# A recurrence with a dense block behind it: TensorE's order of issue mixes two kinds of products, and weights, checks and one inversion move

## The chip, the cores and the metric

The kernel runs on one core of one Trainium2 chip. The metric is the device time of one execution in microseconds (us). Three executions of the kernel before took 703.22, 706.95 and 708.93 us; the median is 706.95 us.

## The reference

For each of 4 batches and 8 heads a 40 x 40 state is carried over 768 time steps; then every token goes through a normalisation and a two-layer block ("MoE" in the names), with a residual:

```
for t in range(768):                       # state: 4 x 8 x 40 x 40, zero at first
    y[t]  = r[t] @ state
    Sa    = state @ a[t]
    state = state * w[t] - outer(Sa, b[t]) + outer(v[t], k[t])
x   = y, heads side by side                # 4 x 768 tokens of 320
xn  = (x - mean) / sqrt(var + 1e-6) * g_ln
out = x + relu(xn @ w_ch1) @ w_ch2         # 320 -> 1280 -> 320
```

All inputs are float32 and so is the output.

## The kernel before, in words

**Chunks.** The 768 steps are cut into 24 chunks of 32 steps. Inside a chunk the recurrence becomes small matrix products per head, all 32 batch-head pairs at once; from chunk to chunk only the state is carried. A chunk's work on TensorE (PE) is a set of small products, each with 32 to 40 columns and often a quarter of the array: `tri` (L424), `pq` (L408) and `kbt` (L531) prepare it, `prh` (L561), `solve` (L576) and `st` (L604) carry the state on, `ss` (L628) and `ut` (L655) transpose, `z` (L672) and `y` (L695) give the chunk's output. VectorE (DVE) runs two scans of the decays per chunk (`g` L367, `q` L376) and evicts results; GpSimd (POOL) scales keys (`kb` L395) and `aT` (L385). The triangular matrices of a slab of 2 or 4 chunks are inverted by forward substitution, row after row (`invert`, L477 to L487): slabs 0 and 1 in two halves of 16 rows on DVE, slab 2 in full on DVE, slabs 3 to 6 in full on POOL. A slab done by halves costs its chunks two more `solve` products and a DVE addition (L583).

**The block.** Two chunks give 256 tokens, a group; there are 12 groups. `norm` makes a group's normalised tokens, split into a high and a low part (transposes `nt`, L878). `moe` runs 10 first products `l1` (L929; 8 matmuls of 256 columns each) and 20 second products `l2` (L906; 3 matmuls of 320 columns each). Between them ScalarE (ACT) writes the high part of the hidden layer (L934) and DVE the low part (L938).

**Weights.** They arrive as 64-bit floats and are turned to a high and a low 32-bit part: ACT shifts the exponent (L748), DVE puts the bits together (L763, L764, L774), POOL multiplies by the sign (L770) and subtracts (L817), in three buffers inside `yi[1]`, the buffer in which POOL later inverts slabs 3 to 6.

**What sets the order.** Every step is a task with its engines, an estimated duration, what it reads and writes, and a due time worked back from the end. `Plan.run` plays all tasks through once before the kernel is built, engine by engine, and always takes the ready task with the smallest key; the result is a fixed list of instructions for each engine. For PE there are two additions. The planner sums an estimate of columns (`USE`) of the products of the last 2.4 planned us; while the sum is under `NEED` (1500) it takes a ready product with over 900 first, which only `l1` and `l2` have. And between 6 and 70 planned us, where nothing is ready, it issues a filler (`unit`, L1048: a product of 160 columns that nobody reads). All DMAs go through SP's queue.

**A check.** `wild` (L362, DVE) collects for each chunk whether any decay lies outside a range; if so, a slow path at the end would redo everything. It isn't taken here.

Of the kernel before, what the change touches and what calls it, by code (L numbers as in the profile page):

```python
# [33 lines left out]
HALVES = (0, 1)  # L34
BY_POOL = (3, 4, 5, 6)
NBK = 7
# [5 lines left out]
SPAN, NEED = 2.4, 1500  # L42
UNITS = (6.0, 70.0)
BACKLOG = 2.0


class Plan:
# [4 lines left out]
    USE = dict(l1=2048, l2=960, nt=384, tri=320, z=320, st=364, prh=480, solve=160, y=520, kbt=100, pq=340, ss=83, ut=80)  # L52
# [7 lines left out]
    def add(self, where, emit, r=(), w=(), shift=0.0, bank=None, of="", kb=0, land=2.2, sort=None, due=None):  # L60

        t = dict(n=len(self.tasks), where=where, emit=emit, shift=shift, due=due, bank=bank, of=of, kb=kb, land=land,
                 deps=set(), sort=sort)
# [16 lines left out]
    def run(self, n_banks=8, unit=None):  # L80
        T = self.tasks
        n = len(T)
        follow = [[] for _ in T]
        left = [0] * n
        uses = {}
        opens = {k: t for t in T for k in t["bank"]}
        for t in T:
            for k in t["ps"]:
                o = opens[k]
                if o is not t:  # L90
                    o["deps"].update(d for d in t["deps"] if d < o["n"])
        for t in T:
            for d in t["deps"]:
                follow[d].append(t["n"])
            left[t["n"]] = len(t["deps"])
            t["uses"] = set()
        for t in T:
            for k in t["bank"]:
                uses[k] = 0
        for t in T:  # L100
            for k in t["ps"]:
                uses[k] += 1
        free = {e: 0.0 for e in self.ENGINES}
        ready = {e: [] for e in self.ENGINES}
        ends = [None] * n
        avail = [0.0] * n
        done = [False] * n
        banks = list(range(n_banks))
        held = {}
        count = {"moe": 0, "po": 0, "small": 0}  # L110
        cap = {"moe": 2, "po": 2, "small": 6}
        wire = [0.0]
        used = []
        events = []
        order = []
        now = 0.0

        def release(t):
            for e, us in t["where"]:
                heapq.heappush(ready[e], (t["key"], t["n"]))  # L120

        for t in reversed(T):
# [5 lines left out]
            late = t["due"] if t["due"] is not None else min((T[f]["late"] for f in follow[t["n"]]), default=END)  # L128
            t["late"] = late - us
            t["key"] = t["late"] + t["shift"]  # L130
        for t in T:
            if left[t["n"]] == 0:
                release(t)
# [1063 lines left out]
```

## Time and profile before

| | us |
|---|---|
| median of 3 runs | 706.95 |
| the profiled execution | 708.33 |
| its span, first to last instruction | 706.2 |
| PE busy | 630.6 |
| DVE busy | 418.3 |
| ACT busy | 297.8 |
| POOL busy | 264.2 |

The profile lists for each engine the time in which at least one of its instructions ran. A busy PE may still be slow: TensorE's clock is granted at one of two levels, 2.4 GHz (1.00 in the rows) or 1.2 GHz (0.50), and the profile gives the mean granted clock of any stretch. Its mean over this execution was 0.788.

### The profile page before, as it was taken

What the parts mean: (1) busy time and instruction counts of PE and PEld (TensorE: products, weight loads), DVE (VectorE), ACT (ScalarE), POOL (GpSimd) and SP (SyncE); (2) the same over time, 40 slices, a digit from 0 to 9 for tenths busy, and PEclk for the clock granted to TensorE, in tenths of its full rate; (3) what the DMA queues carried; (4) which work ended last, traced back from release to release, by engine and by line L of the source; (5) the groups of instructions that cost most, each with busy time, mean ns of one, the idle gap of its engine ahead of it and who ended that gap; (6) DMA issues with size and microseconds to landing.
All of it is one profiled execution on the core that took longest, in us unless ns stands there. A gap on an engine that the chain in (4) does not pass through costs nothing. (4 is left out here: it accounts for less than half of the span.)

```text
span 706.2 us, 29730 instructions
## 1 busy us (share of the span) xinstructions
PE 630.6 (89%) x13026; PEld 585.0 (83%) x13026; DVE 418.3 (59%) x882; ACT 297.8 (42%) x747; POOL 264.2 (37%) x380
## 2 busy tenths in 40 slices
PE   5987788499789999999999899899998998989876
PEld 5987777388678889889889899798898997979866
DVE  8989967978865645563465574474435444354232
ACT  7542356642332742562361552633534534345121
POOL 7653711642169550228462238661156500000000
PEclk9899975559869759756969769588588795896969
DMA  9989758352582883665164681646433434121000
GB/s 198 247 225 242 203 125 164 83 137 69 129 146 65 193 166 88 167 142 147 44 158 107 157 168 49 144 105 145 124 60 96 90 78 97 49 78 44 20 1 21
DMA packets 126646, 84.22 MB, mean 119 GB/s; under 512 B 94896, under 2 KB 104624, under 8 KB 126512
## 3 DMA queue, kind: packets, MB, share of 16 engines
q1 hardware_dynamic: 126512, 82.28, 49.9%
q8 instruction: 103, 1.69, 1.0%
q14 instruction: 31, 0.25, 0.1%
HBM read 56.14 MB, written 18.24 MB: 105 GB/s over the span
## 5 line engine op out<-in xcount | busy, mean ns | idle before, releaser
L938 DVE SCALAR_TENSOR_TENSOR hl<-ps,hh 128x256 fp32r<-128x256 f32 x120 | 50.5, 423 | 123.3 <-ACT hh L934 122.8
L929 PE MATMUL ps<-xh,w 128*128 128x256 f32 x480 | 120.9, 312 | 0.7 <-ACT xh L882 0.6
L934 ACT ACTIVATE hh<-ps 128x256 fp32r<-128x256 f32 x120 | 46.2, 385 | 162.0 <-PE ps L929 158.9
L906 PE MATMUL ps<-w,hh 128*128 128x320 f32 x480 | 109.7, 315 | 0.0
L929 PEld LDWEIGHTS ps<-xh,w 128*128 128x128 f32 x480 | 93.6, 215 | 4.3 <-issue 1.4
L395 POOL TENSOR_TENSOR bk<-bk,gE 112x1024 f32<-112x1024 f32 x24 | 55.7, 2321 | 83.4 <-DVE gE L367 33.1
L906 PEld LDWEIGHTS ps<-w,hh 128*128 128x128 f32 x480 | 79.0, 190 | 0.7
L906 PE MATMUL ps<-w,hl 128*128 128x320 f32 x240 | 74.6, 311 | 0.0
L929 PE MATMUL ps<-xl,w 128*128 128x256 f32 x240 | 73.5, 306 | 0.0
L1048 PE MATMUL ps<-start,ident 128*128 128x160 f32 x376 | 61.1, 322 | 11.3 <-DVE gk L430 6.1
L487 POOL TENSOR_TENSOR yi<-yi,ytmp 128x30 f32<-128x30 f32 (+14 forms) x120 | 67.0, 558 | 9.4
L872 POOL COPY xn<-xn 128x64 f32<-128x64 f32 x15 | 4.7, 312 | 168.5 <-ACT xn L867 167.6
L1048 PEld LDWEIGHTS ps<-start,ident 128*128 128x128 f32 x376 | 57.0, 206 | 12.5 <-DVE gk L430 6.9
L483 POOL TENSOR_TENSOR ytmp<-yi 128x30 f32<-128x30 f32 (+14 forms) x120 | 63.6, 530 | 8.1
L684 DVE TENSOR_TENSOR x5s<-ps,mask 64x256 f32<-64x256 f32 x96 | 40.5, 422 | 29.9 <-PE ps L672 25.0
L614 DVE TENSOR_TENSOR x<-ps,x2s 40x320 f32<-40x320 f32 x92 | 44.9, 488 | 19.2 <-PE ps L604 13.3
L604 PE MATMUL ps<-x,xk 128*40 128x40 f32 (+1 forms) x1472 | 49.7, 238 | 7.0 <-ACT x L591 4.8
L537 ACT COPY xk<-ps 64x320 f32<-64x320 f32 x96 | 40.4, 420 | 32.1 <-PE ps L531 29.4
L604 PEld LDWEIGHTS ps<-x,xk 128*40 128x40 f32 (+1 forms) x1472 | 43.4, 150 | 12.3 <-ACT x L591 7.3
L662 ACT COPY vu<-ps 40x256 f32<-40x256 f32 x96 | 35.2, 367 | 41.4 <-PE ps L655 18.8
L929 PEld LDWEIGHTS ps<-xl,w 128*128 128x128 f32 x240 | 51.8, 216 | 0.3 <-DVE xl L886 0.3
L376 DVE TENSOR_TENSOR_SCAN qE<-wa,last 112x528 f32<-112x528 f32 x24 | 46.7, 1946 | 2.8 <-ACT qc L402 0.9
(118 smaller groups left out, 1227.5 us busy)
## 6 DMA issues: line engine op xcount, KB each, us to landing
wa<-in_et_dram SPq DMA_DIRECT2D x48, 195.2 KB
bk<-in_et_dram SPq DMA_DIRECT2D x48, 192.0 KB
xk<-xk SPq DMA_DIRECT2D x48, 160.0 KB
d_g<-gk SPq DMA_DIRECT2D x48, 128.0 KB
x<-in_vt_dram SPq DMA_DIRECT2D x48, 128.0 KB
d_a<-aT SPq DMA_DIRECT2D x48, 99.0 KB
x2s<-d_a SPq DMA_DIRECT2D x48, 99.0 KB
vu<-in_vr_dram SPq DMA_DIRECT2D x48, 96.0 KB
```

Source lines behind the costliest of these rows:

```text
L376: nc.vector.tensor_tensor_scan(out=flat(qE[R])[:, ::-1], data0=t[R, n:0:-1], data1=flat(last[R])[:, ::-1], initial=0.0, op0=ALU.mult, op1= ...
L395: (nc.gpsimd if e == "POOL" else nc.vector).tensor_tensor(out=kb, in0=kb, in1=gE[R, :, 0:C].unsqueeze(2).broadcast_to([112, 16, 2, C]), op ...
L483: g.tensor_tensor(out=tv, in0=y[:, j + 1:, j:j + 1].broadcast_to([n, m, j]), in1=y[:, j:j + 1, 0:j].broadcast_to([n, m, j]), op=ALU.mult)
L487: g.tensor_tensor(out=yv, in0=yv, in1=tv, op=ALU.add)
L604: nc.tensor.matmul(o[r0:r0 + D, h], lhsT=xk1[FROW[hf], hf, p], rhs=X2[FROW[hf], hf, p, 0:D], start=True, stop=True)
L614: nc.vector.tensor_tensor(out=x2[n][r0:r0 + D, hf, 8 * pp:8 * pp + 8, 0:D], in0=banks[b[name]][r0:r0 + D, 0:CH].rearrange("p (h e) -> p h ...
L684: nc.vector.tensor_tensor(out=x5s[ro:ro + 64, hf, 8 * pp:8 * pp + 8], in0=pz[64 * pp:64 * pp + 64], in1=mask[64 * pp:64 * pp + 64].unsquee ...
L906: nc.tensor.matmul(banks[b[name]][:, 0:CH], lhsT=l[:, us], rhs=ws[f"w2_{f}"][:, y], start=f == 0 and x == 0, stop=f == 9 and x == 2)
L929: nc.tensor.matmul(ph, lhsT=l, rhs=r, start=x == 0, stop=x == 7)
L934: nc.scalar.activation(out=hhs[n], in_=banks[b[name]][:, 0:256], func=AF.Relu)
L938: nc.vector.scalar_tensor_tensor(out=hls[n], in0=banks[b[name]][:, 0:256], scalar=0.0, in1=hhs[n].bitcast(F32), op0=ALU.max, op1=ALU.subtract)
L1048: nc.tensor.matmul(banks[b][:, 0:160], lhsT=ident, rhs=flat(start0)[:, 0:160], start=True, stop=True)
```

## The change: what it does

- **PE's order.** As before, a sum under 1500 takes `l1`, `l2` first. New: a sum over 2500 (`ENOUGH`) takes a ready small product first. In between the key decides. The products `low` (below) count as wide.
- **VectorE's turns with GpSimd.** The planner treats POOL's instructions and some of DVE's (`SHARED`) as users of one port that takes one at a time, and holds a task back until it is free. All chunks may have `aT` and `kb` on DVE or POOL (before: POOL alone from chunk 4 on). A second pass over the plan is written (`PASSES`), but it is set to one.
- **Weights.** The exponent shift goes to PSUM and the bits are put together there; the low part comes from two accumulating products on PE (the weight through the identity or a diagonal of `g_ln`, minus the high part) and an ACT copy. POOL has no part in it any more.
- **Check.** Two ACT instructions per chunk (`far_`) replace `wild`.
- **Slab 2** is inverted by halves (`HALVES`). Slabs 4 and 6 are inverted in `yi[0]` (`BUF`).
- **Fillers** go on to 165 planned us; some loads and clears have an earliest time (`t0`); masks are made with fewer POOL instructions.

PE, late in the kernel (around the seventh group), before: rows of one kernel's order are line, operation, destination and sources, columns; `x_..` is the chunk's state, `ident` a transpose.

```order
L561 MATMUL ps_68<-x_0_90,x2s_92 32x40 x32
L628 MATMUL ps_67<-ident,x_0_90 104x40 x8
L695 MATMUL ps_66<-xk_1_97,x5s 32x40 x32
L576 MATMUL ps_68<-hv_99,tt_111 32x40 x32
L604 MATMUL ps_66<-x_0_90,xk_95 40x40 x16
L655 MATMUL ps_67<-ident,x_0_90 104x32 x8
L655 MATMUL ps_68<-ident,x_0_90 104x32 x8
L604 MATMUL ps_69<-x_0_90,xk_95 40x40 x16
L531 MATMUL ps_70<-ident,bk_83 128x40 x8
L531 MATMUL ps_67<-ident,bk_83 128x40 x8
L878 MATMUL ps_66<-ident,xn_126 128x128 x3
L628 MATMUL ps_68<-ident,x_1_91 104x40 x8
```

The same place in the change (L964 is `l2`; L469, L689, L716, L665 are `pq`, `ss`, `ut`, `st`):

```order
L689 MATMUL ps_67<-ident,x_1_92 104x40 x8
L964 MATMUL ps_72<-w_1_505,hh_134 128x320 x2
L964 MATMUL ps_72<-w_1_505,hl_137 128x320
L469 MATMUL ps_68<-ident,qc 128x104 x4
L964 MATMUL ps_66<-w_2_658,hh_132 128x320 x2
L964 MATMUL ps_66<-w_2_658,hl_135 128x320
L716 MATMUL ps_69<-ident,x_1_92 104x32 x8
L716 MATMUL ps_70<-ident,x_1_92 104x32 x8
L665 MATMUL ps_67<-x_1_92,xk_96 40x40 x16
L665 MATMUL ps_68<-x_1_92,xk_96 40x40 x16
L964 MATMUL ps_72<-w_2_658,hh_132 128x320 x2
L964 MATMUL ps_72<-w_2_658,hl_135 128x320
```

Before, the small products of two chunks stand in one piece, and a group's `l1` and `l2` in another. In the change one or a few `l1` or `l2` stand after every two to five small products.

DVE, slab 2's inversion, before (L483 and L487 are its multiply and add on full rows, L774 and L362 weights and `wild`):

```order
L483 TENSOR_TENSOR ytmp_109<-yi_107 128x58
L487 TENSOR_TENSOR yi_107<-yi_107,ytmp_109 128x29x2
L774 SCALAR_TENSOR_TENSOR yi_108<-r_0_4_844,yi_108 128x256
L367 SCALAR_TENSOR_TENSOR gE<-wa_81,start_79 112x528
L483 TENSOR_TENSOR ytmp_109<-yi_107 128x84
L487 TENSOR_TENSOR yi_107<-yi_107,ytmp_109 128x28x3
L483 TENSOR_TENSOR ytmp_109<-yi_107 128x108
L487 TENSOR_TENSOR yi_107<-yi_107,ytmp_109 128x27x4
L362 SCALAR_TENSOR_TENSOR wild<-wa_82,wild 112x512
L483 TENSOR_TENSOR ytmp_109<-yi_107 128x130
L487 TENSOR_TENSOR yi_107<-yi_107,ytmp_109 128x26x5
```

And in the change (L538, L548 are the multiply and add on halves, L745 and L996 are `z` and the low part of the hidden layer):

```order
L745 TENSOR_TENSOR x5s<-ps_69,mask 64x256
L996 SCALAR_TENSOR_TENSOR hl_136<-ps_72,hh_133 128x256
L538 TENSOR_TENSOR ytmp_110<-yi_108 128x108
L548 TENSOR_TENSOR yi_108<-yi_108,ytmp_110 128x2x9x6
L745 TENSOR_TENSOR x5s<-ps_70,mask 64x256
L538 TENSOR_TENSOR ytmp_110<-yi_108 128x112
L548 TENSOR_TENSOR yi_108<-yi_108,ytmp_110 128x2x8x7
L996 SCALAR_TENSOR_TENSOR hl_137<-ps_68,hh_134 128x256
```

Slab 2 now takes 14 pairs of instructions and not 30, `wild` is gone from between them, and the block's own evictions already run there.

The diff, cut to its core:

```
-HALVES = (0, 1)
+HALVES = (0, 1, 2)
+BUF = (0, 0, 0, 1, 0, 1, 0)
...
-SPAN, NEED = 2.4, 1500
-UNITS = (6.0, 70.0)
+SPAN, NEED, ENOUGH = 2.4, 1500, 2500
+UNITS = (6.0, 165.0)
+SLACK = 0.1
+PASSES, MARGIN = 1, 4.0
...
+    SHARED = ("g", "q", "aT", "kb", "inv", "rs")
...
-                        dry = sum(u for _, u in used) < NEED
-                        for k, i in sorted(q) if dry else ():
+                        use = sum(u for _, u in used)
+                        wide = True if use < NEED else False if use > ENOUGH else None
+                        for k, i in sorted(q) if wide is not None else ():
                             t = T[i]
-                            if not done[i] and avail[i] <= now + 1e-9 and self.USE[t["of"]] > 900:
...
+                            if not done[i] and avail[i] <= now + 1e-9 and (self.USE[t["of"]] > 900) == wide:
+                                if full(t):
                                     continue
                                 got = t
                                 break
...
+                        if port[0] > now + SLACK and (e == "POOL" or e == "DVE" and t["of"] in self.SHARED):
+                            put.append((k, i))
+                            heapq.heappush(events, port[0] - SLACK)
+                            continue
...
+                    if e == "POOL" or e == "DVE" and t["of"] in self.SHARED:
+                        us += max(0.0, port[0] - now)
+                        port[0] = now + us
...
-        def wild_(e, b):
-            (nc.gpsimd if e == "POOL" else nc.vector).scalar_tensor_tensor(
-                out=wild[R], in0=t[R, 0:n].bitcast(U32).rearrange("p (h t) -> p h t", t=33)[:, :, 1:33],
-                scalar=0x3f000000, in1=wild[R], op0=ALU.bitwise_xor, op1=ALU.bitwise_or)
+        def far_(e, b):
+            v = qc[R].rearrange("p (h t) -> p h t", t=C)
+            nc.scalar.activation(
+                out=v, in_=t[R, 0:n].rearrange("p (h t) -> p h t", t=33)[:, :, 1:33], func=AF.Abs, bias=lim[R, 0:1])
+            nc.scalar.activation(
+                out=qc[R], in_=qc[R], func=AF.Relu, bias=lim[R, 1:2], accum_out=far[R, c:c + 1])
...
-        both = [("DVE", 0.72), ("POOL", 1.45)] if c < 4 else [("POOL", 1.45)]
+        both = [("DVE", 0.72), ("POOL", 1.45)]
...
-        u = int(by_pool)
-        yt, tmp = yi[u], ytmp[u]
+        u = BUF[si]
+        yt, tmp = yi[u], ytmp[int(by_pool)]
...
+            def up(e, b):
+                nc.scalar.activation(
+                    out=banks[b[name]][:, 0:n], in_=words(i)[1].bitcast(F32), func=AF.Abs, scale=2.0 ** -111)
+            task("ACT", up, 0.45, r=[("raw", i)], bank=name, of="w")
...
+            def low(e, b):
+                o = banks[b[f"wl{i}"]][:, 0:n]
+                nc.tensor.matmul(o, lhsT=ident if wt else dgs[k], rhs=wf, start=True, stop=False)
+                nc.tensor.matmul(o, lhsT=minus, rhs=ws[tag][:, 0], start=False, stop=True)
+            task("PE", low, 0.8, r=[km, "ident", "gt", "minus", ("wh", tag), ("yi", 1)], bank=f"wl{i}", of="low")
 
             def lo(e, b):
-                t = ws[tag]
-                nc.gpsimd.tensor_tensor(out=t[:, 1], in0=wf, in1=t[:, 0].bitcast(F32), op=ALU.subtract)
-            task("POOL", lo, 0.85, r=[km, ("yi", 1)], w=[("w", tag)], of="w")
+                nc.scalar.copy(out=ws[tag][:, 1], in_=banks[b[f"wl{i}"]][:, 0:n])
+            task("ACT", lo, 0.42, r=[("wh", tag)], ps=[f"wl{i}"], w=[("w", tag)], of="w")
...
```

## Rows read from the trace of the kernel before

**Rows 1.** The page: span, and busy time, share, instructions of three engines.

```profile
span 706.2 us, 29730 instructions
...
PE 630.6 (89%) x13026; PEld 585.0 (83%) x13026; DVE 418.3 (59%) x882; ACT 297.8 (42%) x747; POOL 264.2 (37%) x380
```

**Rows 2.** Three stages: stretch, length, busy us per engine, granted clock, DMA.

```profile
0.00:96.28 96.28, 79.67 (x1336) 75.40 (x1336) 88.10 (x151) 45.51 (x98) 52.87 (x64) 0.96 0.85 214
96.28:161.13 64.85, 49.79 (x1341) 44.19 (x1334) 49.67 (x104) 36.52 (x96) 24.43 (x24) 0.53 0.56 124
161.13:706.20 545.07, 501.10 (x10367) 465.43 (x10366) 280.56 (x629) 215.75 (x554) 186.91 (x292) 0.79 0.44 102
```

**Rows 3.** Same columns: stretches at the low clock after 161 us, eleven in all.

```profile
188.44:205.50 17.06, 10.70 (x171) 9.14 (x172) 12.57 (x41) 6.21 (x15) 5.32 (x14) 0.50 0.85 140
...
290.84:331.80 40.96, 39.30 (x896) 36.14 (x895) 21.24 (x46) 17.91 (x47) 17.99 (x30) 0.50 0.67 154
...
669.72:683.37 13.65, 7.49 (x89) 6.23 (x90) 5.31 (x17) 3.30 (x8) 0.24 (x1) 0.50 0.00 1
sum 228.69, PE 208.64 PEld 186.78 DVE 120.03 ACT 109.37 POOL 70.56; mean PE 18.97 PEld 16.98 DVE 10.91 ACT 9.94 POOL 6.41
```

**Rows 4.** Same columns: stretches at the full clock after 161 us, twelve in all.

```profile
161.13:188.44 27.31, 24.80 (x591) 23.02 (x590) 23.96 (x48) 9.55 (x26) 8.32 (x5) 1.00 0.43 106
...
sum 314.03, PE 292.47 PEld 278.65 DVE 160.53 ACT 106.38 POOL 116.35; mean PE 24.37 PEld 23.22 DVE 13.38 ACT 8.87 POOL 9.70
```

**Rows 5.** PE's timeline: start, duration, instruction; two products, each at both clocks.

```profile
146.30 0.41 PE L929 MATMUL ps<-xh,w1x 128*128 128x256 f32 x1
146.51 0.41 PE L929 MATMUL ps<-xl,w1x 128*128 128x256 f32 x1
...
530.47 0.28 PE L929 MATMUL ps<-xh,w1x 128*128 128x256 f32 x1
530.59 0.28 PE L929 MATMUL ps<-xl,w1x 128*128 128x256 f32 x1
...
539.73 0.80 PE L695 MATMUL ps<-xk,x5s 128*32 128x40 f32 x64
...
555.91 1.29 PE L695 MATMUL ps<-xk,x5s 128*32 128x40 f32 x64
```

**Rows 6.** Fillers alone (L1048): stretch, length, PE busy, PEld busy, clock, DMA.

```profile
78.00:84.00 6.00, 1.71 (x11) 1.23 (x10) 1.00 0.85 281
84.00:96.30 12.30, 5.05 (x32) 4.32 (x32) 1.00 0.45 117
```

**Rows 7.** First products alone (L929), then second products alone (L906), same columns.

```profile
174.80:178.20 3.40, 0.87 (x8) 0.85 (x7) 1.00 0.48 141
...
174.80:178.20 3.40, 1.15 (x6) 0.88 (x6) 1.00 0.48 141
```

**Rows 8.** Groups by line: busy us, mean ns of one, idle before, releasers.

```profile
L362 DVE SCALAR_TENSOR_TENSOR wild<-wa,wild 112x512 uint32<-112x512 uint32 x24 | 19.8, 826 | 0.3 <-DMA wa<-in_et_dram 0.3
...
L483 DVE TENSOR_TENSOR ytmp<-yi 128x30 f32<-128x30 f32 (+14 forms) x30 | 15.4, 515 | 0.2
...
L487 DVE TENSOR_TENSOR yi<-yi,ytmp 64x28 f32<-64x28 f32 (+21 forms) x58 | 21.0, 363 | 2.0
...
L477 DVE TENSOR_TENSOR ytmp<-yi 64x28 f32<-64x28 f32 (+6 forms) x28 | 8.1, 291 | 0.8
...
L402 ACT COPY qc<-qE 104x512 f32<-104x512 f32 x19 | 11.7, 618 | 30.1 <-PE ps L408 15.7 <-DVE qE L376 14.3
```

**Rows 9.** Slab 2's multiplies on DVE: count, ns min/median/max, first and last start.

```profile
L483 DVE TENSOR_TENSOR ytmp<-yi x30: 191/348/1969, 124.1 to 196.7; 128x30 f32<-128x30 f32 x2, 128x58 f32<-128x58 f32 x2, 128x84 f32<-128x84 f32 x2, 128x108 f32<-128x108 f32 x2
```

More of the change, by code (lines that the diff above doesn't have):

```diff
@@ L78, in add, with run @@
         return t["n"]
-    def run(self, n_banks=8, unit=None):
+    def run(self, unit=None):
         T = self.tasks
[L82 to L85, printed above, removed]
         opens = {k: t for t in T for k in t["bank"]}
@@ L91, in run @@
                     o["deps"].update(d for d in t["deps"] if d < o["n"])
+        self.follow = [[] for _ in T]
         for t in T:
             for d in t["deps"]:
[L94 to L120, printed above, removed]
+                self.follow[d].append(t["n"])
         for t in reversed(T):
@@ L127, in run @@
                 us = us * STRETCH + 0.3
-            late = t["due"] if t["due"] is not None else min((T[f]["late"] for f in follow[t["n"]]), default=END)
+            late = t["due"] if t["due"] is not None else min((T[f]["late"] for f in self.follow[t["n"]]), default=END)
             t["late"] = late - us
             t["key"] = t["late"] + t["shift"]
+        best = soon = None
+        self.ends = []
+        for _ in range(PASSES):
+            order, soon = self.lay(soon, unit)
+            end = max(t["end"] for t in T)
+            self.ends.append(round(end, 1))
+            if best is None or end < best[0]:
+                best = end, order, [(t["on"], t["at"], t["end"]) for t in T]
@@ L396, in kb_ @@
                 out=kb, in0=kb, in1=gE[R, :, 0:C].unsqueeze(2).broadcast_to([112, 16, 2, C]), op=ALU.mult)
[L397 to L399 removed]
+        task([("DVE", 1.25), ("POOL", 2.35)], kb_, r=["g"], w=kbk, of="kb")
+        task("ACT", far_, 1.25, r=kw + ["lim"], w=["qc", ("far", c)], of="far")
         def qc_(e, b):
@@ L800, in lo @@
-                def lo(e, b):
-                    for hf, rs in enumerate(rows):
-                        x = w1x[0][:, 640 * hf + CH * i:640 * hf + CH * i + CH]
-                        nc.gpsimd.tensor_tensor(
-                            out=x[64:128], in0=wf[rs], in1=x[rs].bitcast(F32), op=ALU.subtract)
-                task("POOL", lo, 1.7, r=[km, ("yi", 1)], w=[("w", "x", i)], of="w")
+                            nc.scalar.copy(out=x(hf)[rs], in_=x(hf)[0:64])
+                task("ACT", hi, 1.3, r=[km, "gt", ("yi", 1)], w=([("raw", 0), ("raw", 1)] if i == 0 else [])
+                     + [("wh", "x", i)], of="w")
@@ L818, in third @@
-            task("POOL", lo, 0.85, r=[km, ("yi", 1)], w=[("w", tag)], of="w")
-        for i in range(2):
-            first(i)
-            second(i)
-        for i in range(2):
-            third(i)
+                if wt:
+                    nc.scalar.copy(out=t[:, 0], in_=wf)
+                else:
+                    nc.scalar.mul(out=t[:, 0], in_=wf, mul=gt[:, k:k + 1])
+            task("ACT", hi, 0.42, r=[km, "gt", ("yi", 1)], w=[("raw", i), ("wh", tag)], of="w")
+            def low(e, b):
+                o = banks[b[f"wl{i}"]][:, 0:n]
+                nc.tensor.matmul(o, lhsT=ident if wt else dgs[k], rhs=wf, start=True, stop=False)
+                nc.tensor.matmul(o, lhsT=minus, rhs=ws[tag][:, 0], start=False, stop=True)
@@ L827, in weights @@
-            third(i)
+            for _ in one(i):
+                pass
     def norm(g):
```

249 lines of the change are left out of this document (148 added, 101 removed).

## The prediction

> **What bounds the kernel now.** I read the page first [rows 1]: PE is busy in 630.6 of 706.2 us, no other engine in more than 418.3. So PE sets the end, and the question is how fast it runs while it is busy. The busy time of three stages answers that [rows 2]. Up to 96 us DVE is the full engine (88.1 of 96.3 us) and PE runs fillers. From 96 to 161 us the clock is at 0.53 and no engine is full: the first chunks pass through PE, DVE and ACT in turn, while DVE (49.7 of 64.9 us) also inverts slab 2. From 161 us to the end PE is busy in 501 of 545 us, at a mean clock of 0.79. This third stage is the kernel.
>
> The same view, cut where the clock changes, splits it into eleven stretches at 0.50 with 228.7 us, in which PE is busy for 208.6 [rows 3], and twelve at 1.00 with 314.0 us, 292.5 busy [rows 4]. (The few microseconds left are the tail.) The long low stretch from 290.8 to 331.8 us has PE busy in 39.3 of 41.0 us: it isn't idleness that makes it low. What runs in such stretches is the piece of small products of two chunks; the clock comes back with the group's first products. PE's timeline prices the level [rows 5]: the 64 records of one `y` take 1.29 us at 0.50 and 0.80 at 1.00, a ratio of 0.62; the first products start 0.21 us apart at 0.50 and 0.12 at 1.00, a ratio of 0.57.
>
> Where wide and small products alternate, the clock held. From 161.1 to 188.4 us it is full throughout [rows 4]; in one piece of that, 174.8 to 178.2 us, first products take 0.87 and second ones 1.15 of 3.4 us, the rest is small ones [rows 7]. Before 96 us the fillers do the same service: between 78.0 and 84.0 us they fill only 1.7 of 6.0 us, between 84.0 and 96.3 us 5.05 of 12.3, and the clock is 1.00 in both [rows 6]. At 96.3 us they end, and it falls.
>
> **The change part by part.** All sums are against the profiled span of 706.2 us; that execution took 708.3, so 2.1 us lie around the span, and its time is 1.4 us above the median.
>
> *PE's order.* If no low stretch remained after 161 us, the 208.6 busy us in them would shrink by 0.38 of themselves (`y`'s ratio): 79 us, the upper bound. The lower one is no gain from the clock at all, and less than that is a rival below. In the change's order wide products stand after every two to five small ones, but thinner than in the alternating stretch of the trace, where they take 2.0 of 3.4 us: in the rows shown, two small products and one `l2`, and there are places with none for seven or eight small products. I take it that the clock falls in some of them and needs a denser piece to come back, and that a third of the low time stays (about 75 us). Gain: two thirds of 79, **53 us**.
>
> *PE's idle time after 161 us.* It is 20.1 us in the low stretches and 21.5 in the full ones [rows 3, 4]. Of the first, 6.4 us lie in 188.4 to 205.5 and 6.2 in 669.7 to 683.4. The first piece ends when slab 2 comes late: its last multiply starts at 196.7 us [rows 9]. The second is the wait for the last group's normalisation with nothing else left. In the new order nearly two groups of `l1` and `l2` are still to do when the last `y` is issued, and slab 2 is done early, so both have other work over them. I take half of the whole, **21 us**; bounds 0 and 40.
>
> *Slab 2, the check, POOL's weights.* Slab 2 now costs 30 multiplies of 515 ns and 30 adds of about 363 ns on DVE [rows 8], 26 us; by halves it is 14 pairs of about 291 ns each, 8 us. `wild` was 24 times 826 ns, 19.8 us. POOL's weight instructions go, and with them DVE's long cases: a multiply of slab 2 has a median of 348 and a maximum of 1969 ns [rows 9]. After 161 us DVE has room and this is worth nothing by itself. From 96 to 161 us it counts: DVE's busy time is 49.7 of 64.9 us there, and PE's 49.8 busy us at 0.53 would be some 31 under the full clock that the longer fillers bring. The chains from PE to ACT to DVE and back remain. The bounds are 0 and 15 us (64.9 less DVE's 49.7); I take **10**.
>
> *What is added.* Two more `solve` products for each of slab 2's four chunks: 8 at about 0.80 us (they have `y`'s 64 records and 40 columns), **6 us** on a full PE; their copies and additions are covered by `l1` and `l2`. The 24 pairs of `low` replace fillers before 160 us; they cost 0, and if that cover were gone some 13 us, by the filler's 32 records in 5.05 us [rows 6], about 0.16 us each, two records a product of 160 columns, and pairs of 256 to 320 columns. ACT takes 24 times two passes, nearest the copy L402 of 0.62 us [rows 8], 30 us, and some 24 evictions of 0.4 us, 10 us; with 298 us busy now it would be near 340 of some 640 us, so it isn't the bound. Its extra before 130 us can delay the first normalisation; that is inside the 0 to 15. Changing more often between wide and small products costs at most a tenth of a microsecond each time; some fifty more changes, **5 us**. Longer fillers run only where no task was ready in the plan; one that runs late delays a real product by 0.3 us at most each, which I count with those 5.
>
> Sum: 706.2 - 53 - 21 - 10 + 6 + 5 = 633 us of span, and **635 us** with the 2 around it.
>
> **The rivals.**
> *The mix is too thin (the other side).* Then the clock falls between the groups' dense pieces and, what is worse, `l1` and `l2`, which run almost wholly at 1.00 now, are drawn into the low time. The work after 161 us is 292.5 + 0.62 x 208.6 = 422 us at the full clock. With a share f of the busy time low, each us of it doing about 0.57 to 0.62 of the work, it takes 422 / (1 - 0.41 f). With 21 us idle, 11 added and 151 before it, the old 706 is reached at 422 / (1 - 0.41 f) = 523, f = 0.47; the kernel before has 0.42. At f = 0.6 the stage takes 560 and the whole **745 us**. For it: no stretch of the trace has so thin a mix of these very products for long. Against it: the fillers between 78 and 96 us, thinner still in part [rows 6]. Chance 0.12.
> *The chain of chunks becomes the limit.* Each `l1` put between two links of the recurrence delays that link, and PE's list is fixed: where a link is late in fact, everything behind it waits. Then the idle 42 us stay and more of the low time with them, half of it: 706.2 - 40 - 5 + 11 + 2, **674 us**. For it: the plan knows durations only as estimates. Against it: wide work is left until the end, so the chain has slack. Chance 0.13.
> *The clock doesn't follow the order.* If it only followed idleness, the mix would bring none of the 53 us, and the idle time, slab 2 and the additions alone would give 706.2 - 21 - 10 + 11 + 2, **688 us**. The row from 290.8 to 331.8 us, low with 96% busy, speaks against it [rows 3]. Chance 0.05.
> The Trainium skill has that rule: "TensorE: Matmul & The Clock Gate", section "Why this matters for your kernels", says that a drop in throughput is avoided by leaving no idle gaps between bursts of matmuls. By that rule the sum would be the 688 us; the trace doesn't agree, since PE was 96% busy at 0.50, and the measurement decides.
>
> **How the numbers follow.** The forecast, 635 us, is one in which a part of the low time stays; it has a chance of 0.68, and with its bounds it goes from 595 (all 79 us gained, most idle time gone) to 668. Chain 0.13, clock 0.05, too thin 0.12, and 0.02 for nothing moving at all. The range goes from 595 to 695: it takes in the chain and the clock, and leaves out the thin mix, nothing moving, and some 0.05 below 595. About 1% is what a measurement of this kernel can tell from no change. Faster by over 1% (under 700 us): 0.68 + 0.13 + 0.05, 0.86. Slower by over 1%: most of the thin case, 0.11. Within 1%: 0.03.
>
> **What the profile after would show.** The clock after the first `l1` should be full in most stretches, with under 100 us low in all; each group's `l1` and `l2` should be spread over the time of two chunks; `y` should mostly take 0.80 us. PE's idle time after the first `l1` should be near 20 us and not behind slab 2. DVE's busy sum should fall by some 35 us, POOL's too, and ACT's should rise by 30 to 40. The first `l1`, now running at 146 us [rows 5], should come at about 135. The prediction is wrong if the low time is still over 150 us; if PE waits for ACT or DVE within the chain by more than 40 us; or if the first `l1` comes later than 150 us.

## The result, and the profile after

The change makes the kernel faster: four executions took 649.23, 650.84, 658.39 and 659.49 us (median 654.62), beside 702.95 to 708.93 us (median 705.09, four executions) for the kernel before. The ratio is 0.925, 95% interval 0.915 to 0.936. The forecast was 635 us in a range of 595 to 695. Executions of one kernel differ here by 1 to 4% along with the granted clock; the ratios leave the disturbed ones out, so they need not be those of the medians.

The profiled execution took 650.84 us, with a span of 649.1. Of its page, the span, the busy times, the clock in 40 slices and the queue that brings instructions (packets, MB, share):

```profile
span 649.1 us, 30979 instructions
...
PE 591.5 (91%) x13640; PEld 540.3 (83%) x13640; DVE 374.4 (58%) x851; ACT 333.7 (51%) x847; POOL 211.2 (33%) x317
...
PEclk9899898988899887898779999979999998899999
...
q8 instruction: 108, 1.77, 1.2%
```

PE does more instructions (13640 for 13026) in less busy time (591.5 for 630.6 us [rows 1]), and the clock digits stand at 7 to 9 throughout. DVE lost 44 us and POOL 53; ACT gained 36.

The same three stages as [rows 2], same columns (stretch, length, busy per engine, clock, DMA share, GB/s):

```profile
0.00:96.28 96.28, 86.16 (x1217) 77.14 (x1217) 70.55 (x144) 61.94 (x150) 38.31 (x39) 0.95 0.84 214
96.28:161.13 64.85, 57.28 (x1739) 49.76 (x1738) 44.03 (x110) 34.08 (x89) 9.27 (x7) 0.91 0.65 136
161.13:649.10 487.97, 448.05 (x10690) 413.42 (x10689) 259.83 (x598) 237.72 (x609) 163.65 (x271) 0.93 0.52 113
```

The third stage is 57.1 us shorter than the 545.07 of before. In the second the clock is at 0.91 for 0.53 and DVE has 5.6 us less to do. Whether the program is further on by its end, the first `l1` tells. Before, it started at 144.9 us in the trace (the rows at 146 us in the prediction are later records of it; a record is one instruction in the trace); now it starts at 146.5, as PE's first instructions of that line show (count, ns min/median/max, first and last start):

```profile
L987 PE MATMUL ps<-xh,w x2: 415/498/582, 146.5 to 147.1; 128*128 128x256 f32 x2
```

The low stretches after 161 us (as [rows 3]; nine and the tail) and the full ones (as [rows 4]; nine):

```profile
161.00:166.01 5.01, 5.01 (x47) 4.27 (x48) 2.50 (x9) 2.17 (x6) 0.00 (x0) 0.50 0.24 52
...
302.54:316.20 13.66, 11.05 (x204) 9.83 (x192) 5.51 (x11) 6.06 (x15) 11.94 (x22) 0.50 0.72 160
...
sum 64.81, PE 57.23 PEld 51.72 DVE 25.74 ACT 23.66 POOL 21.74; mean PE 5.72 PEld 5.17 DVE 2.57 ACT 2.37 POOL 2.17
```

```profile
428.84:541.48 112.64, 107.21 (x2754) 98.93 (x2753) 64.02 (x155) 63.30 (x162) 43.61 (x81) 1.00 0.59 126
...
sum 423.24, PE 390.95 PEld 361.83 DVE 234.09 ACT 214.19 POOL 141.91; mean PE 43.44 PEld 40.20 DVE 26.01 ACT 23.80 POOL 15.77
```

Busy time at the low clock fell from 208.64 to 57.23 us. At the prediction's 0.38 that is 57.5 us, and the span fell by 57.1. PE's idle time is 423.24 - 390.95 = 32.3 us in the full stretches and 5.8 in the low ones (64.81 - 57.23, less the 1.76 of the tail): 38.1 in all, where [rows 3, 4] have 41.6. So the idle time hardly moved. What ends it did. PE's largest waits after (line, what ended the wait, us in all, times, longest):

```profile
PE ps L637 <- issue: 19.0, 11, 2.6
PE ps L756 <- issue: 5.9, 6, 1.7
PE ps L987 <- issue: 3.6, 3, 1.7
PE ps L485 <- issue: 3.5, 2, 3.1
PE ps L469 <- ACT qc L463: 3.3, 2, 2.6
```

"issue" means that the profile shows nothing that PE waited for. Before, the first of these lines was half as large (L576 is the same product, `solve`):

```profile
PE ps L576 <- issue: 9.6, 8, 2.3
```

Summed over all of PE's gaps of more than 0.25 us in the trace, those without a releaser, called standstills below, rose from 20.9 us (17 gaps) to 35.6 (25), and all others fell from 45.3 us (33 gaps) to 14.1 (10). After 161.13 us alone, standstills rose from 16.6 to 27.3 us and the others fell from 18.8 to 4.8. The timeline shows what a standstill looks like (start, duration, instruction, count, idle before):

```profile
301.61 0.39 PE L987 MATMUL ps<-xh,w1x 128*128 128x256 f32 x1 [1.55 <-issue]
301.83 0.28 PE L987 MATMUL ps<-xl,w1x 128*128 128x256 f32 x1
302.04 0.94 PE L756 MATMUL ps<-xk,x5s 128*32 128x40 f32 x64
302.91 1.28 PE L637 MATMUL ps<-hv,tt 32*32 32x40 f32 x61
306.80 0.34 PE L637 MATMUL ps<-hv,tt 32*32 32x40 f32 x3 [2.61 <-issue]
```

`solve` stops after 61 of its 64 records, which all read the same two tiles, and goes on 2.61 us later. That makes missing data an unlikely cause. Counting PE's records from the start, eight of the 25 lie at the 1496th, 2007th, 2134th, 3789th, 4043rd, 4170th, 8871st and 8998th: steps of 127 or within 4 of a multiple of it. The queue's row says what comes in such portions: 1.77 MB in 108 packets is 16 KiB each, and 13640 matmuls with as many weight loads, 27280 instructions, over 108 is 253. In the trace each of the 25 ends 1.3 to 2.6 us after a packet of that queue has landed. That PE here waits for its own instructions was the theory that the experiments had to test.

The trace also shows what PE did before the clock fell. Each of the nine low stretches began in a gap of PE of 1.55 to 3.06 us or at most 1.5 us after one (above: idle for 1.55 us up to 301.61, and the clock low from 302.54), and eight of these gaps are standstills. Of the 24 gaps over 0.25 us that began at the full clock after the first `l1`, one of 1.77 us and the 14 of less than 1.3 us were not followed by a fall. Before, ten of the eleven low stretches began in a gap or at most 2.3 us after one, with gaps of 0.90 to 2.26 us; the one from 488.81 us began with PE busy in all of the 6.8 us ahead of it. What differs is how long a low stretch lasts: (64.81 - 1.76) / 9 = 7.0 us on average, and 228.69 / 11 = 20.8 before.

### The profile page after: what moved, and what is told of

It reads as the page before. It is cut to its first block, busy times and chain, and to the rows that moved or that the text cites. A ratio compares the mean times of both kernels' runs of the same rounds, so it can differ in the third digit from the quotient of the medians.

```text
span 649.1 us, 30979 instructions
## 1 busy us (share of the span) xinstructions
PE 591.5 (91%) x13640; PEld 540.3 (83%) x13640; DVE 374.4 (58%) x851; ACT 333.7 (51%) x847; POOL 211.2 (33%) x317
## 3 DMA queue, kind: packets, MB, share of 16 engines
q8 instruction: 108, 1.77, 1.2%
## 4 chain that ended last, share of the span: by engine, by line
PE 79%; issue 6%; DMA 6%; DVE 4%; ACT 2%; SPq 1%; POOL 0%; DVEq 0%; POOLq 0%; ACTq 0%
PE ps L987 18%; PE ps L964 17%; PE ps L1107 7%; PE ps L637 5%; PE ps L665 5%; PE ps L733 4%; PE ps L592 3%; PE ps L716 3%; PE ps L485 3%; PE ps L756 3%; PE ps L689 3%; PE ps L622 3%; DMA wa<-in_et_dram 3%; DMA tt<-d_tt 1%; PE ps L469 1%
## 5 line engine op out<-in xcount | busy, mean ns | idle before, releaser
L964 PE MATMUL ps<-w,hh 128*128 128x320 f32 x480 | 119.1, 334 | 0.6 <-DVE hl L996 0.6
L987 PE MATMUL ps<-xh,w 128*128 128x256 f32 x480 | 115.1, 302 | 1.9 <-issue 1.7
L996 DVE SCALAR_TENSOR_TENSOR hl<-ps,hh 128x256 fp32r<-128x256 f32 x120 | 50.5, 422 | 90.0 <-ACT hh L992 89.3
L987 PEld LDWEIGHTS ps<-xh,w 128*128 128x128 f32 x480 | 86.3, 198 | 4.3 <-issue 1.8
L457 POOL TENSOR_TENSOR bk<-bk,gE 112x1024 f32<-112x1024 f32 x21 | 46.1, 2195 | 130.9 <-DVE gE L429 38.9
L964 PEld LDWEIGHTS ps<-w,hh 128*128 128x128 f32 x480 | 79.0, 194 | 6.9 <-issue 2.8
L1107 PE MATMUL ps<-start,ident 128*128 128x160 f32 x402 | 75.4, 340 | 5.6 <-POOL ident masks.py:199 3.1
L964 PE MATMUL ps<-w,hl 128*128 128x320 f32 x240 | 75.7, 315 | 0.0
L1107 PEld LDWEIGHTS ps<-start,ident 128*128 128x128 f32 x402 | 65.6, 216 | 8.8 <-POOL ident masks.py:199 3.1
L548 POOL TENSOR_TENSOR yi<-yi,ytmp 128x30 f32<-128x30 f32 (+14 forms) x120 | 65.3, 544 | 9.4
L745 DVE TENSOR_TENSOR x5s<-ps,mask 64x256 f32<-64x256 f32 x96 | 40.5, 422 | 25.4 <-PE ps L733 23.7
L447 POOL TENSOR_TENSOR aT<-wa,qE 112x512 f32<-112x512 f32 x20 | 25.3, 1267 | 91.2 <-DVE qE L438 68.5
L652 ACT COPY x<-ps 32x320 f32<-32x320 f32 x55 | 22.9, 416 | 49.5 <-PE ps L637 32.1
L964 PEld LDWEIGHTS ps<-w,hl 128*128 128x128 f32 x240 | 46.5, 194 | 0.0
L697 ACT COPY xk<-ps 40x320 f32<-40x320 f32 x92 | 38.6, 419 | 12.6 <-PE ps L689 10.3
```

The source lines that it names most:

```text
L457: (nc.gpsimd if e == "POOL" else nc.vector).tensor_tensor(out=kb, in0=kb, in1=gE[R, :, 0:C].unsqueeze(2).broadcast_to([112, 16, 2, C]), op ...
L548: g.tensor_tensor(out=yv, in0=yv, in1=tv, op=ALU.add)
L697: nc.scalar.copy(out=xk0[i][r0:r0 + D, hf, par::2], in_=banks[b[name]][rp:rp + D, 0:CH].rearrange("p (k e) -> p k e", e=D))
L745: nc.vector.tensor_tensor(out=x5s[ro:ro + 64, hf, 8 * pp:8 * pp + 8], in0=pz[64 * pp:64 * pp + 64], in1=mask[64 * pp:64 * pp + 64].unsquee ...
L964: nc.tensor.matmul(banks[b[name]][:, 0:CH], lhsT=l[:, us], rhs=ws[f"w2_{f}"][:, y], start=f == 0 and x == 0, stop=f == 9 and x == 2)
L987: nc.tensor.matmul(ph, lhsT=l, rhs=r, start=x == 0, stop=x == 7)
```

## The experiments

The kernel before ran beside them on each chip. **Clock theory:** the rule on small products (the sum over 2500) brings the gain, through the clock. Rivals: the other parts bring it; less idle time does. **Supply theory:** in a standstill PE waits for its own instructions, whose supply dense small products outrun.

**The change without the small products first.**

```
-                        wide = True if use < NEED else False if use > ENOUGH else None
+                        wide = True if use < NEED else None
```

> The change with the new half of PE's rule undone: a planned sum over 2500 no longer puts small products first; all else is as in the change. Theory clock (the gain comes from the full clock that the mix keeps): wide products bunch again, the low stretches after the first l1 come back from about 63 us to 150 to 230, and the time is 680 to 700 us. Rival (the gain comes from the other parts: weights off POOL, longer fillers, slab 2 by halves): the time stays within 1.5% of the change's 655 us, and the low time stays under 100 us.

Measured: median 710.23 us (9 executions) beside 703.72, ratio 1.005 [0.999, 1.011]. Its stage after 161 us (to 630), and the sum of its low stretches there, same columns as above:

```profile
161.13:630.00 468.87, 431.44 (x10101) 399.54 (x10103) 238.88 (x538) 210.17 (x538) 163.49 (x278) 0.82 0.53 115
...
sum 203.56, PE 174.13 PEld 156.34 DVE 94.84 ACT 102.03 POOL 50.95; mean PE 14.51 PEld 13.03 DVE 7.90 ACT 8.50 POOL 4.25
```

With this one line undone, the whole gain is gone: the clock is at 0.82 and 174 us of busy time are low again. The low time came back as the theory had it; the time went past its 680 to 700 us. All other parts together are worth nothing that can be measured. Where PE stood still in it, the largest sums:

```profile
PE ps L637 <- issue: 10.7, 10, 2.2
PE ps L689 <- issue: 9.7, 4, 3.9
PE ps L756 <- issue: 9.2, 6, 2.5
```

Its standstills are 34.4 us in 25 gaps, as many as in the change, though its small products bunch again. The clock theory holds.

**Slab 2 whole again.**

```
-HALVES = (0, 1, 2)
+HALVES = (0, 1)
```

> The change with slab 2 inverted in full again on DVE, so without the 8 extra solve products. Theory (halves take slab 2 off the path of chunk 4): some 6 us of PE's idle time come back near 190 to 210 us, less the 6 us of solves not done: 650 to 662 us. Rival (slab 2 was the cause of the slow early part): over 665 us.

Measured: median 669.79 us (4 executions, 662.88 to 677.92), ratio 0.949 [0.941, 0.957]. That is worse than the change in its first comparison (0.915 to 0.936) and overlaps with it in the second, below (0.934 to 0.945). The first `l1` came at 151.3 us. So the halves are worth between nothing and 2.5%, and the runs don't settle it. The time is past the theory's 662 us, and its reason didn't show: PE's idle time is less without the halves (31.3 us after the first `l1`, where the change has 42.0) and the low time more (113.5 us for 69.0, in the profiled execution, the slowest of the four).

**Fillers to 70 planned us only.**

```
-UNITS = (6.0, 165.0)
+UNITS = (6.0, 70.0)
```

> The change with fillers up to 70 planned us as before and not to 165. Theory clock: the clock falls soon after 70 us and stays low until the first l1; small products there run at 0.62 of their pace, first l1 at 155 to 160 us and not 146, the whole 660 to 672 us. Rival (that stretch waits for DVE and for instructions, not for PE's pace): first l1 within 3 us of 146 and the time within 1% of 655.

Measured: 650.96 to 679.94 us in five executions, median 664.98, ratio 0.949 [0.941, 0.956]. The profiled one (span 649.2) equals the change. Its early stage:

```profile
96.28:161.13 64.85, 54.43 (x1749) 47.78 (x1750) 44.48 (x111) 36.21 (x95) 9.30 (x7) 0.76 0.64 136
```

The clock falls to 0.76 from 0.91, and yet the first `l1` comes at 144.5 us, no later than with the longer fillers (146.5) and as the rival had it. The longer fillers hold the clock up there and gain no time by it in that stage. On the whole kernel the spread leaves it open.

**Dense small products alone.** This kernel computes nothing of the reference. PE runs small products of four quarters (`solve`'s shape: 32 products are 64 records) and wide ones (256 columns) without any wait: 40 times 32 small; then 40 times 32 small and 8 wide; then 40 times 32 small and 24 wide.

```
+    for x in range(40):
+        small(x % 4, 32)
...
+    for x in range(40):
+        small(x % 4, 32)
+        wide(4 + x % 4, 8)
```

> A kernel that computes nothing of the reference: PE's instructions alone, with constant operands and the 24 output transfers at the end. First 40 runs of 32 small float32 products (64 records each, 32x40), then the same with 8 wide ones (256 columns) after each run, then with 24. In the change PE stands still in the middle of runs of small products, by 0.4 to 3.1 us, at record counts that differ by multiples of 127 or 128, and a 16 KiB transfer of the instruction queue starts 2 to 3 us before each end. Theory supply (PE's instructions come in blocks of 128 records at no more than one block in about 3.9 us): the first part shows a standstill per 128 records and takes 3.7 to 4.2 us for them, though their own work is 1.6 us at the full clock and 2.6 us at the half; the second has a smaller one or none, the third none. Rival (the standstills come from the kernel's data transfers or from semaphores): with no data transfers and no waits there is no standstill, and 128 records take 1.6 to 2.7 us.

Measured: 330.51 us, span 328.6. PE's timeline in the first part, then in the second:

```profile
16.98 2.35 PE L332 MATMUL ps<-Bm,A 32*32 32x40 f32 x128 [2.44 <-issue]
20.98 2.35 PE L332 MATMUL ps<-Bm,A 32*32 32x40 f32 x128 [1.65 <-issue]
24.71 2.35 PE L332 MATMUL ps<-Bm,A 32*32 32x40 f32 x128 [1.37 <-issue]
28.71 2.35 PE L332 MATMUL ps<-Bm,A 32*32 32x40 f32 x128 [1.65 <-issue]
...
120.72 0.79 PE L332 MATMUL ps<-Bm,A 32*32 32x40 f32 x64
121.44 1.21 PE L336 MATMUL ps<-X,W 128*128 128x256 f32 x8
122.58 0.79 PE L332 MATMUL ps<-Bm,A 32*32 32x40 f32 x64
```

and from its page and its groups by line the queue, and the two kinds of products (busy, mean ns, idle before):

```profile
q8 instruction: 71, 1.16, 1.5%
...
L336 PE MATMUL ps<-X,W 128*128 128x256 f32 x1408 | 193.2, 291 | 0.3 <-issue 0.2
...
L332 PE MATMUL ps<-Bm,A 32*32 32x40 f32 x7680 | 110.3, 218 | 33.0 <-issue 31.5
```

With no other engine at work and nothing to wait for, PE stops after every 128 records, exactly: it runs them in 2.35 us and starts the next 128 only 3.4 to 4.0 us after the last, over all 17 such portions from 16.98 us on (the mean is 3.74; the gaps are of 1.10 to 2.44 us). 9088 records over 71 packets are 128. So a record takes 29 ns of supply (3.74 us over 128) and 18 ns of PE. In the second part 64 small and 8 wide records take 1.86 us (120.72 to 122.58), 26 ns a record, and only five gaps of more than 0.25 us, of 0.69 to 1.23, are left in 40 rounds. From the first of them (100.45 us) to the last (167.01), 2304 records further on, it is again 29 ns a record, now at the full clock. With 24 wide ones there are no such gaps. The supply theory holds for dense small products. The windows of the first part, before and after, with the clock:

```profile
16.78:85.05 68.27, 44.40 (x2285) 41.64 (x2285) 0.00 (x0) 0.00 (x0) 0.00 (x0) 0.50 0.02 4
85.05:150.00 64.95, 61.72 (x2142) 55.27 (x2140) 0.00 (x0) 0.00 (x0) 0.00 (x0) 1.00 0.02 4
```

While PE outran its supply the clock was low (1.2 GHz, from 16.78 us on). It came back at 85.05 us, among the 64 wide products that stand between the two parts, and stayed full.

**The rule alone**, on the kernel before, run twice:

```
-SPAN, NEED = 2.4, 1500
+SPAN, NEED, ENOUGH = 2.4, 1500, 2500
...
-                        dry = sum(u for _, u in used) < NEED
+                        use = sum(u for _, u in used)
+                        wide = True if use < NEED else False if use > ENOUGH else None
...
-                            if not done[i] and avail[i] <= now + 1e-9 and self.USE[t["of"]] > 900:
+                            if not done[i] and avail[i] <= now + 1e-9 and (self.USE[t["of"]] > 900) == wide:
```

> The kernel before with one thing added: a planned sum over 2500 puts ready small products first on PE. Weights on POOL, fillers to 70, slab 2 in full, wild on DVE as before. Theory (the rule carries the whole gain and the other parts are worth nothing together): 645 to 665 us, low time after the first l1 under 110 us instead of 244. Rival (the rule needs the other parts, above all slab 2 by halves and longer fillers, so that small products are ready to mix): 675 to 700 us.

> The kernel before with the rule of 2500 alone, again. Theory (the other parts of the change are worth nothing together): within 1% of the change in this job. Rival (they are worth the 10 to 20 us that the prediction gave them): 1.5% to 3% above it.

Measured: medians 658.68 us, ratio 0.932 [0.917, 0.947], and 655.46 us, ratio 0.928 [0.922, 0.934]. The second was compared on one chip with the change itself (below: 0.939). The early stage and the low stretches after 161 us of the second:

```profile
96.28:161.13 64.85, 49.93 (x1448) 44.04 (x1445) 50.52 (x109) 38.72 (x101) 24.42 (x24) 0.53 0.57 128
```

```profile
sum 90.98, PE 84.75 PEld 77.22 DVE 30.77 ACT 35.29 POOL 46.96; mean PE 9.42 PEld 8.58 DVE 3.42 ACT 3.92 POOL 5.22
```

A few lines of the planner bring the whole gain, and the rest of the change adds nothing to it: where both ran side by side, the rule alone was the faster by its median (655.46 for 661.53 us). Its busy time at the low clock is 123.9 us less than the 208.64 of before; at 0.38 that is 47.1 us, and its span is 51.4 us shorter. Low time after the first `l1` was 113.0 and 104.2 us in the two profiled executions, near the theory's 110. PE's largest waits in the second (L577 is `solve`, L425 `tri`):

```profile
PE ps L879 <- ACT xn L868: 10.3, 4, 6.2
...
PE ps L425 <- issue: 5.2, 2, 2.6
PE ps L577 <- issue: 5.0, 6, 1.3
```

Standstills are 16.8 us there (15 gaps; 19.0 in 15 in the first run), other waits 39.0: the reverse of the change. Standstills thus go with the other parts of the change and not with the order:

| standstills, us (gaps) | without the small-first rule | with it |
|---|---|---|
| other parts as before | 20.9 (17) | 16.8 (15), 19.0 (15) |
| other parts as in the change | 34.4 (25) | 35.6 (25), 30.7 (21) |

The 30.7 us are from the next run. PE's idle time after the first `l1` has the same pattern: 45.6 us before, 33.2 and 36.5 with the rule alone, 52.2 with the other parts alone, 42.0 and 37.0 with both. The seven further versions below and above that have all or most of the other parts show standstills of 23.6 to 37.8 us. Which of the parts does it is not shown.

**The change again**, unaltered, on one chip with the second run of the rule alone and with two versions below.

> The change itself again, on the chip and in the job of the next three, so that they can be held against it: 0.92 to 0.935 of the kernel before, 648 to 660 us.

Measured: 654.88 to 676.59 us in six executions, median 661.53, ratio 0.939 [0.934, 0.945], a little over what was expected. The profiled one has a span of 661.7 and more low time than that above. Its longest low stretch and the sum:

```profile
423.64:454.37 30.73, 30.73 (x520) 27.28 (x521) 12.16 (x32) 13.54 (x35) 5.46 (x7) 0.50 0.38 85
...
sum 98.17, PE 93.49 PEld 85.22 DVE 41.41 ACT 41.34 POOL 31.68; mean PE 10.39 PEld 9.47 DVE 4.60 ACT 4.59 POOL 3.52
```

The same program had 57.23 us of busy time at the low clock in one execution and 93.49 in another. The difference of 36.3, times 0.38, is 13.8 us; the spans differ by 12.6. So between these two executions the difference is the clock's, and the clock term has that uncertainty.

**A denser mix.** `SPAN, NEED, ENOUGH = 2.4, 2200, 3000` in place of 1500 and 2500.

> The change with NEED 2200 and ENOUGH 3000 in place of 1500 and 2500: wide products come more densely where there are any. Theory mix (what low time is left comes from places that are too thin): low time after the first l1 falls from 69 to under 45 us, time 640 to 655 us. Rival (the wide products run out sooner, so a piece of small ones alone is left between groups): low time over 90 us, time 660 to 685 us.

Measured: median 655.67 us, ratio 0.938 [0.927, 0.950]. Low time after the first `l1` is 67.4 us in the profiled execution (span 649.8), as with the change (69.0). No effect either way; neither expectation came.

**The supply written into the plan.** The planner is told how many records each product has, and that PE gets 33 of them a microsecond (30 ns each, near the dense kernel's 29) with up to 200 in hand. In the first version an empty supply also makes it take wide products first; in the second only the planned durations change.

```
+    REC = dict(l1=8, l2=3, nt=3, tri=64, z=64, st=32, prh=64, solve=64, y=64, kbt=8, pq=4, ss=8, ut=8, low=4)
...
+                        have, seen = min(BUFFER, have + (now - seen) * RATE), now
-                        wide = True if use < NEED else False if use > ENOUGH else None
+                        wide = True if use < NEED or have < FEW else False if use > ENOUGH else None
...
+                        us = max(us, (self.REC[t["of"]] - have) / RATE)
```

> The change, and the planner also keeps a count of PE's instruction records that are at hand: up to 200, 33 more per planned us; a product that needs more is planned to take longer, and with fewer than 64 at hand a ready wide product goes first. Theory supply: PE's standstills in the middle of runs fall from 34 us to under 15, and the time to 630 to 648 us. Rival (standstills only move, or wide products are used up early and the later part bunches): standstills fall but the low time rises over 100 us, and the time stays at 650 to 670.

Measured: median 655.64 us, ratio 0.925 [0.908, 0.942]: no different from the change. Standstills fell to 23.6 us, but low time after the first `l1` was 100.9: the rival came.

The second version leaves out `or have < FEW`:

> As x6, but the count only makes planned durations longer; which product goes first is decided as in the change. Theory: the list follows real times better, standstills stay at 25 to 35 us, time within 1% of the change's 655 us. Rival (the order of choice in x6 isn't needed): standstills under 20 us and the same time as x6.

> The change with the supply of instructions in the planned durations, again. Theory supply (a list planned with the real times of dense pieces has its products nearer to when they are ready): 0.5% to 2% under the change in this job, 640 to 650 us. Rival (the one profiled run of it at 639 us was a lucky run): within 0.5%.

Measured: medians 649.45 us, ratio 0.929 [0.919, 0.939], and, on one chip with the repeated change, 645.16 us, ratio 0.912 [0.904, 0.920]. There the intervals stand apart: 0.912 / 0.939 = 0.97. It beats the change and, by the same comparison, the rule alone (0.928 [0.922, 0.934]). The sum of its low stretches after 161 us:

```profile
sum 53.83, PE 50.34 PEld 46.45 DVE 19.52 ACT 19.64 POOL 39.11; mean PE 6.29 PEld 5.81 DVE 2.44 ACT 2.45 POOL 4.89
```

Against the repeated change (span 661.7 to 639.4, 22.3 us) the clock gives (93.49 - 50.34) x 0.38 = 16.4 us, the first `l1` 3.0 (146.0 to 143.0), idle time after it 3.3 (37.0 to 33.7). So most of it is the clock again. Why a plan that knows the supply leaves less low time isn't shown; the standstills themselves fell only from 30.7 to 26.2 us.

**Both: supply in the durations, and a denser mix** (2000 and 2800).

> The same with NEED 2000 and ENOUGH 2800. Theory mix: less low time after the first l1 than the 55 us of the run with the change's thresholds, 632 to 645 us. Rival (wide products run out sooner): 650 us or more.

Measured: 632.09 to 652.76 us in six executions, median 649.77. Low time after the first `l1` fell to 44.0 us in the profiled execution, the least of all, as the theory had it. It has the lowest single time of all and yet a higher median than the version without the denser mix; no ratio can be given, and no difference is shown.

## Why the prediction was right, and which terms were not

The side, the main mechanism and the range were right; the sum was 633 us of span for a measured 649.1. Two terms fell short by 29 us together, and two others made up 13 of that. By its terms:

| term | forecast, us | measured, us |
|---|---|---|
| clock | -53 | -57.5 (0.38 x 151.4); by the repeated execution -43.8 (0.38 x 115.2) |
| PE's idle time after 161 us | -21 | -3.5 (41.6 to 38.1): other waits -14.0, standstills +10.7 |
| first `l1` earlier | -10 | +1.6 (144.9 to 146.5) |
| added work, changes of shape | +11 | +2.3, what is left of -57.1 |

**The clock: right; its size partly by luck.** "A third of the low time stays", 75 us, was an assumption that no row gave: it was 69.0 us after the first `l1` (243.9 before), 109.6 in the repeated execution. That the small-first rule does it is shown by the run without it and by the rule alone. The prediction's rival by which the clock only follows idleness is half right: all nine falls of the change came with gaps, and seven of eight in the repeated execution. But in the repeated change the stretch from 423.64 to 454.37 us is low with PE busy in all of its 30.73 us, after a standstill of 3.06 us. What the rule shortens is the time until the clock is back. After 161 us the kernel before has 11 low stretches of 20.8 us on average, the change without the small-first rule 11 of 18.3, the rule alone 8 of 11.2, and the change 9 of 7.0 and 8 of 11.9 in its two executions. So one step of this term didn't come as written: "I take it that the clock falls in some of them", the thin places of the mix. It fell mostly at standstills, and no run took the standstills away alone to see whether the falls go with them. The rule of the Trainium skill behind that rival ("TensorE: Matmul & The Clock Gate", section "Why this matters for your kernels") agrees with the nine falls of the change, each of which came with a gap, and not with the 30.73 us at the low clock without one.

**PE's idle time: mis-sized, 21 for 3.5.** The step that failed is "both have other work over them ... I take half of the whole". The waits on other engines went as argued: after 161 us they fell from 18.8 to 4.8 us. The term took all of the idle time for such waits. But 16.6 us of it were standstills, a cost that the profile before already showed as "issue" in `solve`'s line and that the prediction never asked about. They rose to 27.3 us, and that took back most of the gain. The new order isn't what raised them, since the rule alone has no more of them than the kernel before; the other parts of the change are, by the table above. By which of them, and why, stays open: how far ahead PE's supply was at any place the trace doesn't show. Since eight of the change's nine low stretches began at standstills, these may cost clock time too; that wasn't tested. The kernel as a whole has 13640 records in 649 us, 48 ns each, against the 29 that the supply took in the dense kernel; so it isn't the mean that stalls but, it seems, dense places such as `y` followed by `solve`, 128 records in about 1.6 us at the full clock (0.80 us for `y` [rows 5], and `solve` taken as the same).

The Trainium skill, "Runtime: NRT & Kernel Launch", section "Instruction fetch mechanics", says that instructions come in blocks of 16 KiB, 256 instructions, fetched ahead, and that crossing a block is mostly hidden, since an engine dispatches more slowly than the fetch fills. The blocks agree with the rows (71 packets for 9088 matmuls and as many weight loads, 1.16 MB); that they are hidden does not hold for dense small products: the gap at each of them was 1.10 to 2.44 us in the dense part. In the change 25 of some 107 showed a gap.

**The first `l1`: nothing for 10.** The step that failed is the one from a better clock and less of DVE to an earlier end of the stage. Both came: the clock in 96 to 161 us rose from 0.53 to 0.91 and DVE fell from 49.67 to 44.03 us. But the first `l1` came at 147.8 us with the rule alone (clock 0.53; 150.6 in its first run), 144.5 with short fillers (0.76) and 146.5 with the change (0.91): it doesn't follow PE's clock, and the lower bound, 0, was the value to take. In the chain of waits of the change between 96 and 147 us every piece is PE's own list, 30.0% of it fillers and 10.7% standstills; but without the longer fillers it came only 2 us earlier, so the links behind them are nearly as late. Which link sets the pace there stays open.

**What is added: perhaps smaller than the 11.** The 2.3 us can't be told from the remainder's own error. The run without the small products first gives a second reading: 706.2, less 0.38 x (208.64 - 174.13) = 13.1, plus 6.6 of idle time after the first `l1` (45.6 to 52.2) and 1.0 for a later first `l1`, is 700.7; it took 705.7, so 5.0 for the additions. One count in the 11 was too low: after 161 us PE changes between `l1` or `l2` and other products 235 times, before 71 times, so 164 more and not some fifty. At the tenth of a microsecond put for each that would be 16 us, and no remainder shows so much.

**The small terms.** DVE's busy time fell by 44 us for "some 35", ACT's rose by 36 for "30 to 40". Slab 2 and the check, as these groups by line show, cost what the working had (42 multiplies and 42 adds on DVE for 58 [rows 8], two ACT passes for `wild`), and the runs show nothing of it in the whole time:

```profile
L425 ACT ACTIVATE qc<-qc,lim 112x512 f32<-112x512 f32 x24 | 17.3, 723 | 0.8
L423 ACT ACTIVATE qc<-wa,lim 112x512 f32<-112x512 f32 x24 | 17.3, 722 | 20.1 <-DMA wa<-in_et_dram 9.6 <-PE ps L469 6.5 <-PE ps L1107 2.0
...
L548 DVE TENSOR_TENSOR yi<-yi,ytmp 64x28 f32<-64x28 f32 (+13 forms) x42 | 13.0, 308 | 1.4
...
L538 DVE TENSOR_TENSOR ytmp<-yi 64x28 f32<-64x28 f32 (+13 forms) x42 | 9.9, 235 | 1.1
```

One reading behind that term was only partly right: it put DVE's long multiplies of slab 2 down to POOL's weight instructions. In the trace of the kernel before the three longest (1969, 1606 and 1365 ns) overlap POOL's `kb`, `kb` and `aT`; beside its weight instructions are ones of 1021 and 686 ns. Two long ones (2247 and 1196 ns) are left among the change's halves.

**The rivals.** Too thin a mix needed a low share f of 0.47; it was 57.23 / 448.05 = 0.13. The chain as the limit had half a point: most of the idle 42 us stayed, as it said, but as standstills and not as waits in the chain, and the low time didn't stay with them. That the clock doesn't follow the order is refuted, as far as the length of the low stretches goes, by the run without the small products first.

## What to carry to other kernels

When an engine's busy time is long because its clock is low, cost the order of its instructions first and by itself: here a few lines of a planner were worth 7%, and all the other edits beside them nothing that could be measured. Before promising idle time back, list what ends each gap; those in the middle of one product, without a releaser and at a fixed step in the count of instructions, point to the supply of instructions, and here removing the other waits didn't remove them. Look at what the engine did before each fall of its clock, and cost the falls and the time until it is back apart. Run each part alone: the order by itself left less idle time than the whole change. And run the final kernel twice: one program gave spans of 649 and 662 us, with 57 and 93 us of busy time at the low clock.

## What the runs showed of the hardware

PE's instructions arrived in packets of 16 KiB, 128 matmuls with their weight loads, and in a stretch of nothing but 32 x 40 products the next packet's worth started 3.4 to 4.0 us after the last, though PE ran each in 2.35 us. At 1.2 GHz PE was busy for the whole of a stretch of 30.73 us, wide and small products mixed, and the clock came back only at its end. It fell, in all nine low stretches of the change after 159 us, in or at most 1.5 us after a gap of 1.55 to 3.06 us; in the dense kernel it came back among wide products and stayed at 2.4 GHz through gaps of 0.69 to 1.23 us.
